# Waiting for the output stores on GpSimd instead of SyncE in a linear-attention block

## The chip, the cores and the metric

The kernel runs on one core of a Trainium2 chip. A core has a matrix engine (TensorE, PE in the profile, with its weight loads as PEld), a vector engine (VectorE, DVE), a scalar engine (ScalarE, ACT), a general engine (GpSimd, POOL) and SyncE (SP), which has no arithmetic and issues DMAs and waits. Each engine has an instruction stream of its own, and the streams meet only through semaphores: counters that one side raises and the other waits for. A "q" behind an engine's name in the profile (SPq, POOLq) is what its sequencer does itself: DMA issues, waits, drains.

The metric is the device time of one execution in microseconds (us). Lower is better.

## What is computed

A block of linear attention for a sequence of 2048 rows and a width of 640, with 32 heads of 20 columns, in bf16:

```python
qkv = (x @ wqkv).reshape(B, S, 3, H, Dh)      # B=1, S=2048, D=640, H=32, Dh=20
phi = lambda t: jnp.where(t > 0, t + 1, jnp.exp(t)) + 1e-6
pq, pk = phi(q), phi(k)
kv  = einsum("bhsd,bhse->bhde", pk, v)         # one 20x20 state per head
z   = einsum("bhsd->bhd", pk)
num = einsum("bhqd,bhde->bhqe", pq, kv)
den = einsum("bhqd,bhd->bhq", pq, z) + 1e-6
out = (num / den).reshape(B, S, D) @ wo
```

## The kernel before

The program is written out instruction by instruction and fully unrolled. `Plan.add` (L36) notes an operation for one engine, with the buffers that it reads and writes, and works out which semaphores it has to wait for. `Plan.emit` (L78) then writes one engine's list into that engine's stream, each operation behind its waits. Each DMA has a semaphore of its own, which stands at 16 when its data have landed; each engine has one that counts its finished operations.

The work goes through these stages. The rows of x come in plain (`xn`) and transposed (`xT`), the weights beside them, nearly all issued from SP. K is computed for 16 tiles of 128 rows (`k_half`, L293) and put through phi (`k_phi`). The state is built with x in place of v (`p_step`, L317), so that v is never formed; Q is computed in tiles of 512 columns (`q_tile`, L354); the per-head state is masked and multiplied with `wo` (`kv_group`, L445; `w2_mm`, L472). The denominators go through a logarithm and an exponential on ACT and are spread over the partitions by DMA (`den_spread`, L561), and DVE multiplies Q with them (`normalize`, L569). The order of all this is one handwritten string of letters at L722.

The last stage is the output. For each tile of 128 rows, `out_tile` (L605) multiplies on PE into two PSUM banks (`out_mm`, L576), ACT and DVE copy the banks into one of four SBUF buffers `osb` (`out_evac`, L599 and L602), and `out_dma` (L585) stores the tile, 128 rows by 640 columns, from SP. The sixteenth tile is cut smaller (`out_last`, L612): of its four column pieces the first two, columns 0 to 480, are stored together from SP (120 KB), and the last two, columns 480 to 640, from ACT (40 KB). So there are 17 stores for 16 tiles, and `out_keys` lists them.

GpSimd has little to do: it fills the identity matrix and the masks at the start (L154 to L174), and builds `zb` for the denominators with five small multiplications (L433). It issues no DMA.

When all five streams have been written (L727 to L729), a loop (L730 to L732) adds one wait for each of the 17 stores. These are the last instructions of the program; nothing of the kernel stands behind them. They make sure that the program doesn't end before its output has landed.

Of the kernel before, what the change touches and what calls it, by code (L numbers as in the profile page):

```python
# [84 lines left out]
def bass_standalone__linear_attn_block__prompt_kernel(nc, x, wqkv, wo, out):  # L85
# [15 lines left out]
    with contextlib.ExitStack() as ctx:  # L101
# [38 lines left out]
        P = Plan(nc, es)  # L140
# [588 lines left out]
            P.emit(name, eng)  # L729
        for key in out_keys:  # L730
            op = P.writers[key]
            nc.sync.wait_ge(P.sem_obj[op.sem], op.val)  # L732


# [26 lines left out]
```

## Time and profile before

Three runs took 99.40, 99.43 and 99.69 us, so the median is 99.43 us. The profile is of one execution, which took 99.56 us by the same clock.

| | profiled execution |
|---|---|
| time | 99.56 us |
| span, first to last recorded instruction | 98.3 us |
| time around the span | 1.26 us |
| PE busy | 95.1 us, 97% of the span |
| DVE busy | 63.7 us, 65% |
| ACT busy | 48.8 us, 50% |
| POOL busy | 4.7 us, 5%, 19 instructions |
| clock granted to TensorE | 1.000 |
| read from and written to HBM | 5.90 MB and 2.62 MB |

How to read it: times in the views count from the span's first instruction. The chain that ended last is followed back from the last instruction, at each step to what released it. The semaphore waits of a sequencer aren't counted as busy time; their rows show how long they took to execute once they were satisfied, and not how long they stood. The time around the span is what the execution spends before the first and after the last recorded instruction.

### The profile page before, as it was taken

How to read it: one execution, taken by the hardware profiler on the slowest of the kernel's cores; microseconds unless marked ns; L12 is line 12 of the kernel's file. 1: busy time of each engine (PE TensorE's matmuls, PEld its weight loads, DVE VectorE, ACT ScalarE, POOL GpSimd, SP SyncE). 2: the span in 40 equal slices, each digit the busy share in tenths (PEclk: the TensorE clock that was granted, in tenths of full speed). 3: DMA queues.
4: the chain of work that ended last, by engine and by line, in shares of the span. 5: the costliest groups of instructions: out<-in, count | busy, mean ns of one | idle time of the engine just before them, and what ended most of it. 6: DMA issues, size and time to landing. Idle time of an engine off the chain costs nothing.

```text
span 98.3 us, 1814 instructions
## 1 busy us (share of the span) xinstructions
PE 95.1 (97%) x694; PEld 61.2 (62%) x699; DVE 63.7 (65%) x124; ACT 48.8 (50%) x93; POOL 4.7 (5%) x19
## 2 busy tenths in 40 slices
PE   6999999999999999999999999999999999999991
PEld 2467777777755444445687867655557677777771
DVE  5314998888899439997839836758999206272222
ACT  5116455544526120005806456796988765453532
POOL 6500000000000000000000520000000000000000
DMA  2999999999998294000340023313200335532334
GB/s 48 320 269 194 238 157 111 350 366 360 316 169 108 21 239 80 0 0 0 63 77 7 0 63 93 94 32 86 79 0 0 133 74 168 205 117 87 130 133 137
DMA packets 26369, 12.60 MB, mean 128 GB/s; under 512 B 18553, under 2 KB 26361, under 8 KB 26361
## 3 DMA queue, kind: packets, MB, share of 16 engines
q1 hardware_dynamic: 25640, 11.87, 50.2%
q10 hardware_dynamic: 720, 0.61, 1.9%
q8 instruction: 5, 0.08, 0.3%
q14 instruction: 4, 0.02, 0.1%
HBM read 5.90 MB, written 2.62 MB: 87 GB/s over the span
## 4 chain that ended last, share of the span: by engine, by line
PE 95%; ACT 2%; issue 0%
PE ps L293 23%; PE ps L576 22%; PE ps L354 22%; PE ps L317 21%; PE ps L283 3%; ACT w2g L483 2%; PE ps L445 1%; PE ps L544 1%; PE ps L200 1%; PE ps L472 1%; ACT osb L599 0%
## 5 line engine op out<-in xcount | busy, mean ns | idle before, releaser
L317 PE MATMUL ps<-pk,xn 128*128 128x480 bf16 (+1 forms) x160 | 23.2, 299 | 0.0
L293 PE MATMUL ps<-wk,xT 128*128 128x320 bf16 x160 | 22.8, 303 | 0.0
L354 PE MATMUL ps<-xT,wqn 128*128 128x512 bf16 x95 | 22.0, 379 | 0.4 <-issue 0.2
L576 PE MATMUL ps<-w2p,pq 128*128 128x320 bf16 (+2 forms) x170 | 22.1, 291 | 0.0
L293 PEld LDWEIGHTS ps<-wk,xT 128*128 128x128 bf16 x160 | 15.6, 98 | 6.8 <-DMA wk<-in_wqkv_dram 0.9
L576 PEld LDWEIGHTS ps<-w2p,pq 128*128 128x128 bf16 x170 | 15.9, 98 | 6.2 <-issue 0.2
L317 PEld LDWEIGHTS ps<-pk,xn 128*128 128x128 bf16 x160 | 13.6, 98 | 9.4 <-issue 0.3
L362 ACT ACTIVATE eq<-ps 128x512 bf16<-128x512 f32 x20 | 11.9, 597 | 13.8 <-PE ps L354 13.6
L354 PEld LDWEIGHTS ps<-xT,wqn 128*128 128x128 bf16 x100 | 11.5, 118 | 9.1 <-issue 0.3
L306 ACT ACTIVATE ek<-ps 128x640 bf16<-128x640 f32 x16 | 11.2, 704 | 10.7 <-PE ps L293 10.1
L599 ACT CAST osb<-ps 128x320 bf16<-128x320 f32 (+2 forms) x27 | 11.0, 413 | 9.7 <-PE ps L576 9.0
L311 DVE SCALAR_TENSOR_TENSOR pk<-ps,ek 128x640 bf16<-128x640 f32 x16 | 13.2, 825 | 0.5
L569 DVE TENSOR_TENSOR pq<-pq,rd 128x512 bf16<-128x512 bf16 x20 | 7.3, 418 | 4.2 <-DMA rd<-rdc 4.2
L375 DVE TENSOR_SCALAR eq<-eq 128x512 bf16<-128x512 bf16 x20 | 5.8, 288 | 5.9 <-ACT eq L362 5.8
L602 DVE CAST osb<-ps 128x320 bf16<-128x320 f32 (+1 forms) x7 | 3.2, 456 | 8.7 <-PE ps L576 8.7
L308 DVE TENSOR_SCALAR ek<-ek 128x640 bf16<-128x640 bf16 x16 | 5.2, 325 | 5.3 <-ACT ek L306 5.1
L366 ACT ACTIVATE rq<-ps 128x512 bf16<-128x512 f32 x13 | 7.7, 592 | 0.0
L339 ACT CAST pt<-ps 128x480 bf16<-128x480 f32 x4 | 2.2, 562 | 8.2 <-PE ps L317 8.1
L379 DVE TENSOR_TENSOR pq<-eq,rq 128x512 bf16<-128x512 bf16 x13 | 5.5, 426 | 1.1 <-ACT rq L366 0.7
L388 DVE TENSOR_TENSOR za<-pk 128x1280 f32<-128x1280 bf16 x4 | 5.8, 1482 | 0.0
L382 DVE SCALAR_TENSOR_TENSOR pq<-ps,eq 128x512 bf16<-128x512 f32 x7 | 4.8, 692 | 0.2
L388 DVE TENSOR_TENSOR za<-za 128x1280 f32<-128x1280 f32 x3 | 4.4, 1486 | 0.0
(37 smaller groups left out, 36.7 us busy)
## 6 DMA issues: line engine op xcount, KB each, us to landing
out_dram<-osb SPq DMA_DIRECT2D x15, 160.0 KB, 1.8
xn<-in_x_dram SPq DMA_DIRECT2D x2, 640.0 KB, 8.9
xn<-in_x_dram SPq DMA_DIRECT2D x1, 960.0 KB, 7.0
wqn<-in_wqkv_dram SPq DMA_DIRECT2D x1, 800.0 KB, 5.6
wv<-in_wqkv_dram SPq DMA_DIRECT2D x5, 150.0 KB, 5.1
wog<-in_wo_dram SPq DMA_DIRECT2D x2, 375.0 KB, 5.3
w2p<-w2g SPq DMA_DIRECT2D x10, 75.0 KB
rd<-rdc SPq DMA_DIRECT2D x8, 64.0 KB, 2.1
```

The lines of the kernel that those rows point to most:

```text
L293: r = e.matmul(bank(b + h, HALF), xT[:, c * S + 128 * st:c * S + 128 * st + 128], wk[:, c * D + HALF * h:c * D + HALF * (h + 1)], start=(c ...
L306: P.add("act", lambda e: e.activation(fold(t[:, :]), two_banks(b), ACTF.Exp), reads=banks + ["table"], writes=[("ek", st % 3)])
L311: P.add("dve", lambda e: e.scalar_tensor_tensor(fold(pk[:, st * D:(st + 1) * D]), two_banks(b), 0.0, fold(t[:, :]), ALU.max, ALU.add), rea ...
L317: return e.matmul(bank(d // PB[h], PW[h], off=PW[h] * (d % PB[h])), xn[:, st * D + 128 * d:st * D + 128 * d + 128], pk[:, st * D + PO[h]:s ...
L354: r = e.matmul(bank(b), wqn[:, d * D:(d + 1) * D].rearrange("p (q c) -> p c q", c=NC_)[:, c, :], xT[:, d * S + BK * sbk:d * S + BK * (sbk ...
L362: P.add("act", lambda e: e.activation(t[:, :], bank(b), ACTF.Exp), reads=[("bank", b), "table"], writes=[("eq", i)])
L366: P.add("act", lambda e: e.activation(r[:, :], bank(b), ACTF.Relu), reads=[("bank", b), "table"], writes=[("rq", i)])
L375: P.add("dve", lambda e: e.tensor_scalar(t[:, :], t[:, :], 1.0, 1e-6, ALU.min, ALU.add), reads=[("eq", i)], writes=[("eq", i)])
L388: P.add("dve", lambda e: e.tensor_tensor(d_ap, a, b, ALU.add), reads=ra + rb, writes=[dst])
L569: P.add("dve", lambda e: e.tensor_tensor(v, v, rd[i][:, BK * h:BK * (h + 1)], ALU.mult), reads=[("rd", i, 2 * h), ("rd", i, 2 * h + 1), (" ...
L576: r = e.matmul(bank(b, hi - lo), pq[:, c * S + 128 * st:c * S + 128 * st + 128], w2p[:, c * D + lo:c * D + hi], start=(c == 0), stop=(c == ...
L599: P.add("act", lambda e: e.copy(osb[j][:, lo:hi], bank(b, hi - lo)), reads=[("bank", b)], writes=keys)
```

## The change

The loop that ends the program names another engine:

```diff
@@ -729,7 +729,7 @@
             P.emit(name, eng)
         for key in out_keys:
             op = P.writers[key]
-            nc.sync.wait_ge(P.sem_obj[op.sem], op.val)
+            nc.gpsimd.wait_ge(P.sem_obj[op.sem], op.val)
```

The 17 waits now stand at the end of GpSimd's stream, behind the last of its five multiplications for `zb`. SyncE's stream ends with its last DMA issue. The DMAs, their queues, their semaphores and all operations of the other engines stay where they were.

## Prediction

> **What bounds the kernel now.** I read the page's engine shares first, then the chain that ended last, then the end of the timeline.
>
> ```profile
> span 98.3 us, 1814 instructions
> PE 95.1 (97%) x694; PEld 61.2 (62%) x699; DVE 63.7 (65%) x124; ACT 48.8 (50%) x93; POOL 4.7 (5%) x19
> PE 95%; ACT 2%; issue 0%
> ```
>
> PE is busy from end to end and makes 95% of the chain. The change touches no PE instruction, and no operation that PE waits for, so everything up to the last store should stay where it is. What is left is the tail:
>
> ```profile
> 96.34 0.02 issue
> 96.36 0.23 ACT osb L599
> ```
>
> ```profile
> 96.00 0.58 ACT L599 CAST osb<-ps 128x160 bf16<-128x160 f32 x2 [1.28 <-PE ps L576]
> 96.67 0.35 ACTq L587 DMA_DIRECT2D out_dram<-osb  x1
> ```
>
> ```profile
> 97.00:98.00 1.00, 0.00 (x0) 0.00 (x0) 0.00 (x0) 0.00 (x0) 0.00 (x0) 1.00 0.56 164
> ```
>
> The first fence is the end of the chain, the second the end of the timeline, the third a window of 1 us after it. The last arithmetic ends at 96.59 us, the last store is issued from ACT at 96.67, and from 97 to 98 us no engine computes (five zeros) while the DMA engines are 56% busy. The span ends at 98.3 with the waits that the change moves:
>
> ```profile
> L732 SPq EVENT_SEMAPHORE  x9: 17/28/28, 96.8 to 98.3; - x9
> ```
>
> ```profile
> SPq L732 <- DMA out_dram<-osb: 0.5, 1, 0.5
> ```
>
> ```profile
> out_dram<-osb SPq DMA_DIRECT2D x1, 120.0 KB, 1.7
> out_dram<-osb ACTq DMA_DIRECT2D x1, 40.0 KB, 1.6
> ```
>
> The first is what the source line of the waits did: nine instructions (one wait for one store, eight for two: 1 + 16 = 17), 17 to 28 ns each once satisfied, the last starting at 98.3. The other two are SP's waits and the landings. The last store was issued at 96.67 and lands 1.6 later: 98.27. The 120 KB store, issued at 96.36, lands at about 98.06. So SP ends 0.03 us after the last landing. The landing sets the end, and not the number of waits: SP goes through seven of the nine while the last two stores fly.
>
> **The change, part by part.**
>
> *What leaves SP.* Nine instructions, 17 + 8 x 28 = 241 ns. Seven of them lie beside the last two flights, and behind them SP has nothing of the kernel to issue: its last DMA issue is at 96.36. No store goes earlier or later. Gain: 0, hidden by the 1.6 us flight. Without that cover they would cost 0.24 us.
>
> *What POOL gets.* The same 17 waits, behind its last work:
>
> ```profile
> 55.23 1.94 POOL L433 TENSOR_SCALAR zb<-hm,zc 128x32 bf16<-128x32 bf16 x5 [51.26 <-DVE zc L428]
> ```
>
> This is POOL's timeline from 50 us on: it ends at 57.17. After that it is free for 41 us, issues no DMA, and nothing is queued behind the waits. So it stands at each store's wait before the store lands, and late waits can't pile up: only the last two are open after 98.06, some 0.2 us apart, against at most 28 ns each by SP's row. If a wait on POOL were as slow as its slowest sequencer row (169 ns, below), the two would still fit nearly into that gap and the flight. The span should then end at 98.3 + 0.00 to 0.17, and I take 0.03 or less: POOL's own two waits at the start (line 746) took 17 ns each, as SP's did.
>
> *What follows the last wait.* The run took 99.56 us, 1.26 more than its span. The trace's records of semaphore steps, which no view prints, show what happens there. After the engines' last instructions one semaphore takes nine steps, at 96.50, 97.30, 97.33, 97.38, then 98.44, 98.48, 98.52, 98.55, 98.60 us. I read this as a roll call: five engines sign on in a fixed order, then it is passed back through the four others. PE's last matmul ends at 96.32 (sign 1 at 96.50), ACT's last issue at 97.02 (sign 2 at 97.30), SP's last wait at 98.30 (sign 5 at 98.44). POOL and DVE, both long done, must be signs 3 and 4; their order isn't shown. So today the last to finish is also the last in the list, and after SP's sign only four short steps remain: 98.44 to 98.60, 0.16 us.
>
> With the waits on POOL, the one that finishes last stands third or fourth. After its sign the call must go on to SP and only then back. The same pattern runs twice more with nobody late: before the first instruction (third to last step: 44 + 23 + 113 + 38 + 34 + 47 = 299 ns) and after the one above (44 + 23 + 99 + 38 + 34 + 47 = 285 ns). Against SP's 163 ns that is **122 to 136 ns more** if POOL is third, 78 to 92 if it is fourth (44 less). I take 0.11 us.
>
> The Trainium skill ("Runtime: NRT & Kernel Launch", section "The ~15µs preamble/postamble breakdown") describes a closing barrier of about 1.5 us that waits for all engines, and a serpentine of 44 ns a hop over eight hops. Read as one fixed barrier it speaks against my term: whoever comes last, the sum would be +0. By its hop price the two further hops would be an estimate of +0.09. The steps of this trace, 23 to 113 ns, decide.
>
> *POOL's own turn from wait to sign.* No row shows it. SP needed 98.30 to 98.44 = 0.13 us, PE 96.32 to 96.50 = 0.18, ACT 97.02 to 97.30 = 0.27. A reason for POOL to be slower is in the rows of the program's start:
>
> ```profile
> L746 SPq DRAIN  x1: 7/7/7, 0.0 to 0.0; - x1
> L746 POOLq DRAIN  x1: 169/169/169, 0.4 to 0.4; - x1
> ```
>
> POOL's drain took 169 ns where SP's took 7, though POOL then still had fills running. Bounds: -0.13 (POOL signs at once) to 0.14 + 0.16 = +0.30 (a turn like ACT's and a drain like its first). I take +0.07, half of the way to ACT's, since an idle POOL has little to drain.
>
> **Sum.** 0 (SP) + 0 (span) + 0.11 (longer roll call) + 0.07 (POOL's turn) = +0.18 us: 99.74 against the profiled execution's 99.56. That execution lies 0.13 above the median of the runs, 99.43, so I name **99.61** for the median. Bounds of the sum: 0.08 - 0.13 = -0.05, and 0.17 + 0.14 + 0.30 = +0.61.
>
> **The rivals.** About 0.3%, 0.3 us, is what a measurement of this kernel can tell from no change, and the cases are divided there.
>
> A. *The forecast*: 99.5 to 99.73, likeliest 99.61. Not told from no change by itself. Chance 0.42.
>
> B. *Slower: POOL's turn is expensive.* POOL drains and signs late: 0.14 for the call, 0.16 for a drain like the first, 0.14 for a turn like ACT's = +0.44, so 99.87. It decides from a turn of about 0.13 + 0.17 = 0.30 us on (with the call's 0.13, together 0.30). For it: POOL's drain row, and that POOL's arithmetic rows are several hundred ns for little work (388 ns for 32 columns, 1.94 / 5). Against it: POOL will have been empty for 41 us, and its two semaphore rows are as short as SP's. Chance 0.38.
>
> C. *Nothing reaches the metric.* Either the metric ends before the roll call, or the waits cost the same on both. 99.43. Against it: 1.26 us lie around the span, and the call's end at 98.60 is only 0.3 of them. For it: no view shows where the metric starts and stops. That the waits are left out altogether would be a special form, with a span ending at 97.0 and the roll call ending before the output lands; nothing supports it. Chance 0.10.
>
> D. *Faster: SP's tail is on the path.* The time from 94 us on has one transfer of instructions:
>
> ```profile
> q14 instruction: 1, 0.01, 0.4%
> ```
>
> The trace puts it at 98.17 us, 0.31 us long, just after SP's second-last wait. If this is SP's closing code, and the time behind the span waits for it, an SP that is done at 96.7 fetches it in the shadow of the stores: up to -0.31, so 99.12. Against it: SP signs at 98.44, before that transfer ends at 98.48, so the sign doesn't need it. Chance 0.10.
>
> **How the numbers follow.** Predicted: case A, 99.61. Range 99.30 to 100.00: it takes in A, C, the lower bound -0.05 with the spread of the three runs, and B up to +0.57; it leaves out most of D (0.09) and the top of B (0.08). Slower by over 0.3%: B, 0.38. Within 0.3%: A and C, 0.52. Faster by over 0.3%: D, 0.10.
>
> **What would show it.** In the profile after: the nine wait instructions under POOLq, the first soon after the first store's landing, the last at about 98.3; no SP wait after 96.7; PE's share, the chain, the stores' issue and landing times unchanged to a few hundredths; among the semaphore steps, two or three held back to the end in place of one, with sign 3 or 4 late and about 0.29 us from it to the last. A turn over 0.3 us between POOL's last wait and its sign would be B. A span that grows by over 0.2 us, or waits that start late one behind the other, would refute the part on POOL's waits. A last matmul that isn't at 96.3 us would mean that something ahead of the tail moved, which I have no reason for. The prediction is wrong, too, if the last step comes 0.1 us later and the time doesn't follow.

## The result and the profile after

The changed kernel took 100.45 us (median of 7 runs, 100.19 to 101.0), the kernel before 99.59 us beside it (7 runs, 99.4 to 99.92). The ratio is 1.0084, with a 95% interval from 1.0061 to 1.0107. So the change costs about 0.84 us, and not 0.18. The kernel before itself lies 0.16 us above the 99.43 that the forecast started from; that part of the miss is not the change's. Runs more than 1.5% above the fastest of their kernel are left out of the ratios, spans, bands and means here and below.

First the page and the source line of the waits, after:

```profile
span 98.7 us, 1819 instructions
PE 95.0 (96%) x699; PEld 60.9 (62%) x699; DVE 63.7 (65%) x124; ACT 48.7 (49%) x93; POOL 4.7 (5%) x19
```

```profile
L732 POOLq EVENT_SEMAPHORE  x9: 17/43/43, 89.5 to 98.7; - x9
```

The nine wait instructions stand under POOLq now. The first fires at 89.5 us, when its store has landed, and the last at 98.7, right behind the last landing, as forecast; those for two stores take 43 ns where SP's took 28. Work and busy time are those of before. The end of the timeline and the landings:

```profile
96.41 0.58 ACT L599 CAST osb<-ps 128x160 bf16<-128x160 f32 x2 [1.28 <-PE ps L576]
97.08 0.35 ACTq L587 DMA_DIRECT2D out_dram<-osb  x1
```

```profile
out_dram<-osb SPq DMA_DIRECT2D x1, 120.0 KB, 1.7
out_dram<-osb ACTq DMA_DIRECT2D x1, 40.0 KB, 1.6
```

The landings take 1.7 and 1.6 us as before. The whole output stage lies 0.41 us later (97.08 against 96.67). The chain shows where that comes from:

```profile
1.18 0.06 issue
1.24 3.72 DMA wk<-in_wqkv_dram
4.96 0.05 issue
5.00 0.31 PE ps L293
5.87 21.64 PE ps L293 x158
```

In the chain of the kernel before, the same long stretch of PE starts 0.43 us sooner, and no load stands ahead of it:

```profile
5.44 21.66 PE ps L293 x158
```

At the start of the changed kernel's execution a weight load landed late, and PE waited for it. The change touches nothing there. Over many runs the spans of the two kernels are alike: 98.57 us on average in the 7 runs after, 98.54 in 34 runs of before on the chip of the first experiments. What differs is the **time around the span**, time less span, of each run:

| kernel | runs | time around the span, us | mean |
|---|---|---|---|
| before | 34 | 1.21 to 1.33 | 1.26 |
| after | 7 | 1.79 to 2.20 | 1.97 |

So 0.71 of the 0.84 us lie outside the recorded span, and the spans themselves show no difference. (They are known to 0.1 us, so a single value is good to 0.05.) The only witnesses behind the last recorded instruction are the trace's records of semaphore steps, which no view prints. Times in us; "turn" is from the end of the last wait to that engine's sign in the roll call, "call" from there to the call's last step:

| profile | last landing | last wait ends | sign | turn | call ends | call |
|---|---|---|---|---|---|---|
| before (SP) | 98.260 | 98.304 | 98.436 | 0.132 | 98.599 | 0.163 |
| after (POOL) | 98.665 | 98.733 | 99.265 | 0.532 | 99.549 | 0.284 |

The third step is the one that moved to the end: POOL signs third. From landing to the end of the call it is 0.339 us before and 0.884 after: 0.024 more to the end of the wait, 0.400 for the turn, 0.121 for the call, +0.545 in all. Together with the 0.41 us of the late start that makes 0.95, and the two profiled executions differ by 0.94 us (99.56 and 100.5). The start is luck, and the runs lose 0.84, so something behind the call was still missing.

### The profile page after: what moved, and what is told of

Same layout as the page of the kernel before. It is cut to its first block, busy times and chain, and to the rows that moved or that the text cites. A ratio compares the mean times of both kernels' runs of the same rounds, so it can differ in the third digit from the quotient of the medians.

```text
span 98.7 us, 1819 instructions
## 1 busy us (share of the span) xinstructions
PE 95.0 (96%) x699; PEld 60.9 (62%) x699; DVE 63.7 (65%) x124; ACT 48.7 (49%) x93; POOL 4.7 (5%) x19
## 4 chain that ended last, share of the span: by engine, by line
PE 93%; DMA 4%; SPq 0%; DVE 0%; issue 0%; ACT 0%
PE ps L293 22%; PE ps L576 22%; PE ps L317 22%; PE ps L354 22%; DMA wk<-in_wqkv_dram 4%; PE ps L445 1%; PE ps L544 1%; PE ps L472 1%; SPq L241 0%; DVE xT L212 0%; ACT osb L599 0%; PE ps L200 0%
## 5 line engine op out<-in xcount | busy, mean ns | idle before, releaser
L293 PE MATMUL ps<-wk,xT 128*128 128x320 bf16 x160 | 22.2, 299 | 0.9 <-DMA wk<-in_wqkv_dram 0.8
L354 PE MATMUL ps<-xT,wqn 128*128 128x512 bf16 x100 | 23.1, 379 | 0.0
```

Of the source, the lines that this page charges most:

```text
L293: r = e.matmul(bank(b + h, HALF), xT[:, c * S + 128 * st:c * S + 128 * st + 128], wk[:, c * D + HALF * h:c * D + HALF * (h + 1)], start=(c ...
L354: r = e.matmul(bank(b), wqn[:, d * D:(d + 1) * D].rearrange("p (q c) -> p c q", c=NC_)[:, c, :], xT[:, d * S + BK * sbk:d * S + BK * (sbk ...
```

## Experiments

**Theory 1**: only the engine that finishes last counts, by its turn and its place in the call. **Theory 2**: the waits that stand on POOL for 41 us disturb the run itself. The edits below replace the loop at L730; the rest is the kernel before.

**The changed kernel again.**

> The changed kernel once more, unaltered, to see which of its differences come again. In the profile pair, 0.94 us divides into 0.41 us ahead of the last matmul (a weight load that landed later at the start) and 0.52 us between POOL's last wait and the end of the roll call (0.40 for POOL's turn from wait to sign, 0.12 for the longer call). Theory 1, the tail alone is due to the change: the ratio is about 1.005 to 1.006 (+0.52 us), the turn is again 0.5 to 0.55 us, and the last matmul lies anywhere between 96.1 and 96.6 us. Theory 2, the standing waits on POOL disturb the start or the whole run as well: the last matmul is again 0.3 to 0.5 us later than 96.12, and the ratio is about 1.009.

Measured: 100.64 us (median of all 11 runs), ratio 1.0083 (1.0055 to 1.011). Turn 0.532, call 0.285. In this profile the last matmul ends at 96.91, later than before's 96.32, but over the runs the span is 98.57 us against 98.54. So the ratio is the one that theory 2 named, but not for its reason: the span doesn't grow. The time around it is 1.83 to 2.24 us, mean 2.05 (9 runs): 0.79 more than before, where theory 1 explains 0.54. Neither theory was enough.

**15 stores waited for on POOL, the last two on SP.**

```diff
         for i, key in enumerate(out_keys):
             op = P.writers[key]
-            nc.sync.wait_ge(P.sem_obj[op.sem], op.val)
+            eng = nc.sync if i >= len(out_keys) - 2 else nc.gpsimd
+            eng.wait_ge(P.sem_obj[op.sem], op.val)
```

> The waits for the first 15 stores stand on POOL, those for the last two stores on SP. POOL has then 15 of the 17 standing waits, and SP is the one that finishes last. Theory 1 (only the last to finish counts): the time of before, ratio 0.998 to 1.002; roll call from SP's sign to its end 0.16 us; POOL signs at its turn, since its last wait (for the store that lands at about 97.1 us) is over about 1 us earlier. Theory 2 (the standing waits on POOL cost by themselves): +0.3 to +0.4 us, as ahead of the last matmul in the changed kernel's profile.

The source line of this kernel's waits:

```profile
L733 POOLq EVENT_SEMAPHORE  x8: 17/43/43, 88.1 to 97.6; - x8
L733 SPq EVENT_SEMAPHORE  x1: 28/28/28, 98.6 to 98.6; - x1
```

Measured: ratio 1.0007 (0.9981 to 1.0033). Eight of the nine wait instructions stand on POOL and cost nothing that the ratio can tell, and the span, 98.57 us on average, is as long as before's 98.54. So theory 2 falls. POOL's turn is again 0.532 us (97.649 to 98.181), but SP signs at 98.749, behind it, with a turn of 0.137 and a call of 0.163. The time around the span, though, has a new spread: 1.23 to 1.61 us, mean 1.39, where before has 1.21 to 1.33.

**One store, the last, waited for on POOL; 16 on SP.** The edit is that of the last kernel with `nc.gpsimd if i >= len(out_keys) - 1 else nc.sync`.

> The waits for the first 16 stores stand on SP, that for the very last store alone on POOL. Theory 1: all of the tail comes with this one wait: turn of POOL 0.5 to 0.55 us, call 0.28 us, so +0.5 us against before, ratio about 1.005, and the same as the changed kernel but for what lies ahead of the last matmul. Theory 2 (cost per wait on POOL, or of the many standing waits): close to the time of before, ratio below 1.002.

```profile
L733 SPq EVENT_SEMAPHORE  x8: 28/28/28, 96.6 to 98.0; - x8
L733 POOLq EVENT_SEMAPHORE  x1: 17/17/17, 98.2 to 98.2; - x1
```

Measured: ratio 1.0042 (1.0019 to 1.0064); turn 0.542, call 0.285; time around the span 1.77 to 1.85, mean 1.80. One wait on POOL brings the whole 0.54 us. But this is narrow and 0.25 below the changed kernel, which differs from it in two things: SP has no waits at all, and POOL has eight more. So the missing part belongs to SP's shorter stream or to POOL's longer one; which of them, this run can't tell.

**All waits on DVE.** `nc.vector` in place of `nc.sync`.

> All 17 waits stand on DVE, which signs fourth if POOL is third. Theory 1 with a price by position: the call from DVE's sign to its end takes 0.24 us (0.28 less the 0.044 of one step), 0.08 more than from SP's; DVE's turn has no row yet, and lies between SP's 0.13 and ACT's 0.27: in all +0.05 to +0.25 us, ratio 1.0005 to 1.0025, clearly less than with POOL. Rival (any engine other than SP pays the same, since SP's is the only short turn): a turn of 0.5 us as on POOL, +0.45 us, ratio about 1.0045.

Measured: ratio 1.0024 (1.0003 to 1.0045). Turn 0.140, call 0.242, as worked out from the place. From landing to the end of the call it is 0.460 us, 0.121 more than before, but the time around the span is 1.33 to 1.77 us, mean 1.57: 0.31 more. Again a wide rest of about 0.2, again with no wait on SP.

**Where the rest goes: theory F.** The records of instruction transfers show it. In the window of the kernel before, from 98 to 102 us:

```profile
DMA  0100000000000000000000000000000000000000
...
q14 instruction: 1, 0.01, 0.5%
```

and in that of the changed kernel's second profile:

```profile
DMA  9996000000000000000000000000300000000000
...
q14 instruction: 1, 0.01, 0.9%
```

Each digit is 0.1 us. A transfer is drawn in the slice where it starts. Before, the one transfer of 8 KB stands in the second slice (98.17 to 98.48 us by its record), at the eighth wait on SP, while the last store flies. After, the digits on the left are stores, and the transfer is the single 3 on the right: 100.88 to 101.45, behind the whole closing. The same holds for the waits split 15 and 2 (99.91 to 100.45) and those on DVE (100.06 to 100.49). In these three profiles the time is the end of the transfer less 0.29 to 0.31 us (101.45, 100.45, 100.49 and 101.14, 100.14, 100.20). In the other ten profiles, that of the change among them, it is the last step on the roll call's semaphore (98.60 is not the last: the call runs once more, 1.15 us later) less 0.18 to 0.19 us. The time follows whichever comes later. The test is to give SP its instructions back, with no part in the end:

```diff
         for i, key in enumerate(out_keys):
             op = P.writers[key]
-            nc.sync.wait_ge(P.sem_obj[op.sem], op.val)
+            nc.gpsimd.wait_ge(P.sem_obj[op.sem], op.val)
+            if i < len(out_keys) - 1:
+                nc.sync.wait_ge(P.sem_obj[op.sem], op.val)
```

> All 17 waits on POOL as in the changed kernel, and the waits for the first 16 stores on SP as well, where they are long satisfied and hold nothing up: SP only has its eight wait instructions back. Theory F: SP's shorter stream moves one instruction transfer of SP (8 KB, about 0.3 to 0.57 us) from the flight of the last stores to the end of the closing part, where it costs 0 to 0.45 us, differently in each run (time around the span 1.79 to 2.24 us in the changed kernel). With the eight instructions back the transfer starts at SP's eighth wait, near 98 us, and the time around the span is 1.77 to 1.85 us in every run, as with the split of 16 and 1; ratio 1.0045 to 1.006, the tail of POOL's turn and call (+0.54 us) alone. Rival G: the spread comes from POOL, whose closing work varies once all nine waits stand there: around the span 1.8 to 2.2 us again, ratio 1.008.

```profile
L734 SPq EVENT_SEMAPHORE  x8: 28/28/28, 96.7 to 98.1; - x8
```

```profile
DMA  2000000000000000000000000000000000000000
...
q14 instruction: 1, 0.01, 0.7%
```

The first is the source line of SP's waits, the second the window from 98 to 102 us. The transfer is back in the first slice, at SP's eighth wait, and the time around the span is 1.77 to 1.80 us in all five runs, mean 1.78. Theory F holds, and G (POOL's own closing varies) falls. The ratio doesn't follow: 1.009 (1.0064 to 1.0116) where 1.0045 to 1.006 was expected, because the spans of these five runs average 98.74 us against 98.43. That part isn't the tail; it is taken up below.

**The same with DVE**: `nc.vector` in place of `nc.gpsimd` in that edit.

> All 17 waits on DVE and the waits for the first 16 stores on SP as well. Theory F: the time around the span falls from 1.33 to 1.77 us (waits on DVE alone) to a narrow 1.35 to 1.42 us: 1.26 of before and 0.12 for DVE's wait, turn and place in the call; ratio 1.001 to 1.0015. Rival G: 1.33 to 1.77 us again, ratio 1.0024.

Measured: time around the span 1.29 to 1.41 us, mean 1.34, against 1.33 to 1.77 without SP's instructions. The spread goes here too. Ratio 1.0022 (0.9997 to 1.0048), again with longer spans, 98.64 against 98.43.

**All waits on ACT**: `nc.scalar` in place of `nc.sync`.

> All 17 waits on ACT, second in the call. By the steps measured so far the call from ACT's sign to its end takes 0.28 + 0.04 = 0.32 us, 0.16 more than SP's. ACT's turn was 0.27 us behind its last store issue; if that is its turn, +0.14 more; if only 0.14 us as DVE's is, +0.01. SP's stream is as short as in the changed kernel, so the transfer costs 0 to 0.45 us more. In all +0.17 to +0.75, middle +0.4 us, ratio about 1.004, with a wide spread of the time around the span. If POOL's 0.53 us were what every engine but SP and DVE pays, the ratio would be 1.007 to 1.009.

Measured: ratio 1.004 (1.0018 to 1.0063); turn 0.110, call 0.321; time around the span 1.37 to 1.86, wide, as for every kernel without waits on SP. The 0.27 us that the prediction took for ACT's turn stood behind a DMA issue; behind a wait it is 0.110.

**All waits on PE, with SP's 16**: `nc.tensor` in that edit.

> All 17 waits on PE, which signs first, and the waits for the first 16 stores on SP as well, so that SP's transfer of instructions stays early. By the steps measured so far the call from PE's sign to its end takes 0.32 us from the second sign on and one more step of 0.03 to 0.04, in all 0.36 us, 0.19 to 0.20 more than from SP's; turn 0.11 to 0.18 us. Theory of places and turns: time around the span 1.42 to 1.52 us, narrow; ratio 1.002. Rival (the place costs little, POOL alone is special): 1.25 to 1.35 us, as before.

Measured: turn 0.186, call 0.358; time around the span 1.48 to 1.55, mean 1.53, a little above the expected band; ratio 1.0033 (1.0004 to 1.0063). So the places are now measured for all five: PE 0.358, ACT 0.321, POOL 0.285, DVE 0.242, SP 0.163.

**What POOL's turn is not.** Three kernels, all with 17 waits on POOL and 16 on SP. The first has two drains of the empty POOL, one ahead of the waits for the last two stores, one at the end:

```diff
+            if i == len(out_keys) - 2:
+                nc.gpsimd.drain()
             nc.gpsimd.wait_ge(P.sem_obj[op.sem], op.val)
...
+        nc.gpsimd.drain()
```

> As the kernel with 17 waits on POOL and 16 on SP, with two explicit drains on POOL, both of an empty engine: one ahead of the waits for the last two stores, one behind the last wait. They measure what a drain of an idle POOL takes, and what it adds at the end. Theory H: POOL's turn of 0.53 us, 0.40 more than SP's, is a drain that POOL does before it signs: each explicit drain takes 0.17 to 0.45 us, and the second lengthens the way from the last wait to the sign by about as much, to 0.75 to 1.0 us. Rival I: the turn is something else (fetch of closing code, slow sequencer steps): an idle POOL's drain takes under 0.05 us and the sign comes 0.55 to 0.65 us after the last wait.

```profile
L733 POOLq DRAIN  x1: 46/46/46, 97.5 to 97.5; - x1
```

```profile
L737 POOLq DRAIN  x1: 34/34/34, 98.6 to 98.6; - x1
```

An idle POOL drains in 46 and 34 ns, by these two source lines; the 169 ns of the program's start were measured with fills still running. From the second drain's end to the sign it is 0.525 us. Theory H (a drain) falls. Ratio 1.0067 (1.0042 to 1.0092).

The second puts a fill on POOL just ahead of the last wait:

```diff
+            if i == len(out_keys) - 1:
+                nc.gpsimd.memset(hm[:, :], 0.0)
             nc.gpsimd.wait_ge(P.sem_obj[op.sem], op.val)
```

> 17 waits on POOL and 16 on SP, and a fill of POOL's long unused mask behind the wait for the 16th store, so that POOL has computed 0.2 us before its last wait. Theory J: the turn of 0.53 us comes of POOL having stood idle for 41 us: the turn falls to 0.15 to 0.35 us. Theory K: the turn is what POOL's closing steps always take: 0.52 to 0.55 us again, time around the span 1.75 to 1.85 us. A turn of 0.6 to 0.8 us would say that the closing waits for the fill.

Measured: the fill runs to 98.595, the wait ends at 98.546, the sign is at 99.108: 0.562 us behind the wait and 0.513 behind the fill. An engine that has just worked doesn't sign sooner, so theory J (idleness) falls. Ratio 1.0079 (1.0044 to 1.0113), time around the span 1.73 to 1.81.

The third repeats all 17 waits on POOL behind a drain:

```diff
+        nc.gpsimd.drain()
+        for key in out_keys:
+            op = P.writers[key]
+            nc.gpsimd.wait_ge(P.sem_obj[op.sem], op.val)
```

> 17 waits on POOL and 16 on SP, then a drain and the same 17 waits once more on POOL, all satisfied by then. It gives POOL's pace through steps that wait for nothing. Theory L: POOL's sequencer is slow for each step, and the closing is a few such steps: its waits follow each other at 0.12 us or more, the span grows by 1.1 us or more. Theory K: they follow at 0.06 to 0.08 us as on SP (0.07), the span grows by 0.55 to 0.75 us, and the turn behind the last of them is again 0.52 to 0.55 us, so that it lies in closing steps that only POOL has.

```profile
L738 POOLq EVENT_SEMAPHORE  x9: 17/43/43, 98.5 to 99.2; - x9
```

Measured: the repeated waits follow each other every 0.087 us (98.568, 98.654, ... 99.174 by their records), between what theories K and L named, where SP goes at 0.070. The turn behind them is 0.526 us, the ratio 1.0195 (1.011 to 1.028). POOL is a quarter slower for each step; at its pace, 0.40 us would be about five steps more than SP has. Whether the closing has such steps can't be seen: it leaves no instruction in the trace.

A fetch of POOL's closing code can be looked up. In the changed kernel's first profile, from 97 to 102 us, only these two queues moved anything, and neither is one of instructions:

```profile
q1 hardware_dynamic: 221, 0.20, 12.4%
q10 hardware_dynamic: 144, 0.04, 3.4%
```

POOL's turn lies inside this window (98.733 to 99.265 us) and is 0.532 us all the same. So no recorded transfer of instructions makes it.

## Why the prediction was wrong, point by point

- *The span and PE's chain stay*: right. The waits fire as the stores land, and don't pile up. The span is 98.57 us on average against 98.54; the 0.41 us in the profile pair is a late weight load.
- *The roll call gets longer*: right in place and size. POOL is third; the call took 0.284 us after its sign (forecast 0.29), 0.121 more than SP's, forecast 0.11 with 0.122 to 0.136 for the third place. With DVE, ACT and PE the price by place came out as worked out ahead of each run, within 0.01 us.
- *POOL's own turn from wait to sign*: this step failed in size. It was put at +0.07, with +0.30 as its upper bound; it measured 0.53 us against SP's 0.13, **+0.40**, and in all seven profiles with POOL last it lies at 0.51 to 0.54 us, counted from POOL's last recorded instruction; 0.53 also where POOL was done early. The bound was built of a drain of 169 ns, which takes 34 to 46 on an idle POOL, and of ACT's 0.27, which stood behind a DMA issue. Neither row was about the thing to be priced. Rival B named this way and its price, 0.44 us for turn and call together, came close to the 0.52 measured. That the price came close is luck: of its parts, the drain is excluded by the runs, and ACT's own turn behind a wait is 0.110 us.
- *What leaves SP, gain 0*: this step failed altogether. The seven waits beside the flights are hidden, as said, but SP's eighth wait also stands where an 8 KB instruction transfer begins. Without the waits the transfer starts up to 2.7 us later (98.17 and 100.88 us) and costs from 0 to 0.45 us, **0.17 to 0.25 on average** (1.97 and 2.05 us less the 1.80 of the kernel with 16 waits on SP).
- *Rival D* had the right object and the wrong sign: the transfer lay in the shadow of the stores before, and it is the change that takes it out of there.
- *Rival C* (nothing reaches the metric) falls: in ten of the thirteen profiles the time keeps a constant distance, 0.18 to 0.19 us, to the last step of the closing, and in the other three to the end of the late transfer, so what stands behind the span counts.

The sum as measured: 0.02 (wait) + 0.40 + 0.12 + 0.17 to 0.25 = 0.71 to 0.79 us. The time around the span grows by 0.71 (7 runs) and 0.79 us (9 runs); this is no second witness for the sum, since the last term was taken from it. The first three come from the steps alone, 0.54, and the 16 and 1 split confirms them with 1.80 - 1.26 = 0.54. The rest up to 0.84 lies within the interval, 0.61 to 1.07 us.

The Trainium skill ("Runtime: NRT & Kernel Launch", section "Instruction fetch mechanics") says that an engine's instructions are refilled in blocks of 16 KiB by its own DMA queue and that a crossing is mostly hidden. The five transfers on the profile's other instruction queue, q8, have that size (0.08 MB, so 16 KB each); that they are PE's is likely, but no row names the engine. The one here is 8 KB, and with SP's waits gone it isn't hidden in every run; the measurement decides.

**What stays open.** What POOL does in its 0.53 us: drain, idleness, the number of its waits and a recorded transfer of instructions are excluded, and a pace of 0.087 us a step makes it only with some five steps more than SP has, which no record shows. And the span of some kernels that had waits on two engines: 98.74, 98.61 and 98.73 us on average in three with POOL's 17 and SP's 16 (alone, with the drains, with the fill) and 98.64 with DVE's 17, against 98.43 or 98.42 for before beside them, but 98.43 against 98.42 with PE's 17 and SP's 16. They carry little new but waits, behind the last store or on an engine that is idle otherwise, and the span of one kernel varies by over 1 us from run to run (98.1 to 99.3 in 34 runs of before). In all thirteen profiles it is 1.93 to 2.00 us from the end of the last matmul to the last landing, so what makes a profiled span long stands ahead of the last matmul, as the late weight load did above. Four kernels out of five with a longer span speak against chance alone, but I can't say whether the 0.2 to 0.3 us are those kernels' own. For the kernels with all 17 waits on POOL, what SP's 16 bring back therefore shows in the time around the span alone, and not in the ratio (1.009, 1.0067 and 1.0079 against 1.0084).

## What to carry to other kernels

What stands behind the last recorded instruction is part of the time, and which engine finishes last helps to set it: time less span, compared over many runs, shows it at once, before any view does. The last wait belongs on the engine that closes fastest, here SP, which signs 0.13 us after its wait and stands last in the call; from the landing to the end of the call any other took 0.12 to 0.54 us more. And a wait that is hidden can still do something useful: moving it moved an instruction transfer out of its cover.

## What the runs showed of the hardware

- The closing is a call in fixed order (PE, ACT, POOL, DVE, SP, then back). It is read from the steps of one semaphore: with each of the five engines last in turn, the late step stood at that engine's place. From a sign to the call's end it took 0.358, 0.321, 0.285, 0.242 and 0.163 us with that engine last. The turn from wait to sign took 0.186, 0.110, 0.526 to 0.562 (with no drain between them), 0.140 and 0.132 to 0.137.
- POOL goes through waits that are already satisfied at one each 0.087 us, SP at 0.070.
- SP fetched 8 KB of instructions at the same place of its stream in each profile with eight or nine waits on it, within 0.08 us of the start of its eighth wait; with one or none the transfer came 1 us or more behind the last landing, or wasn't recorded.
